# Block-diagonal product in a linear-attention kernel: 16 full matmuls replaced by four groups of 32x32 tile matmuls, woven into the last two q units

## Chip, cores and metric

One core of a Trainium2 chip. The metric is device microseconds of one execution of the whole program; 1 us of this program is 0.06%.

Three kinds of number appear. *Time* is a run's measured time. *Span* is that of the profiled run. *Stretch* is the distance between two instructions inside one trace. Several executions of one kernel differ by up to 1.5 us in time. A stretch repeats within about 0.03 us. Where less than 1.5 us is argued, the stretch is what counts. A *bubble* is time in which TensorE waits, and a *pack* is a group of 16 small matmuls that work side by side.

## The reference, cut to what matters

Two kinds of block alternate, attention (A) and a gated product (B), twice each. Only A is touched.

```python
def _A_ref(x, wqkv, wo):              # B, S, D = 1, 2048, 1024; H = 32 heads of Dh = 32
    qkv = ...                         # x @ wqkv, split by head
    pq, pk = phi(q), phi(k)
    kv = einsum("bhsd,bhse->bhde", pk, v)      # one 32x32 matrix per head
    num = einsum("bhqd,bhde->bhqe", pq, kv)
    den = ...
    return (num / den as B, S, D) @ wo
```

The kernel does not form `num`. It folds each head's 32x32 `kv` into that head's 32 rows of `wo`, giving M (1024x1024), and multiplies the normalised q by M. M is the product of a block-diagonal matrix with `wo`. Below, a q unit computes q for one tile of 128 rows, and an output unit multiplies one tile of the normalised q by M. TensorE writes to PSUM, which other engines must empty; a bank is a [128, 512] fp32 piece of it.

## The kernel before

`both` issues two matmuls, one for each half (512 columns) of a 1024-column output.

```python
def both(ps, lhsT, rhs, start, stop):
    for n in range(2):
        nc.tensor.matmul(out=ps[:, n, :], lhsT=lhsT, rhs=rhs[:, n * NB:(n + 1) * NB], start=start, stop=stop)

def g_unit(m):                     # G = xn^T phi(k), one block of 128 rows
    def run():
        ps = mm_tile()             # [128, 2, 512] fp32 in PSUM, two banks; three such buffers
        for t in range(NT):
            both(ps, XN[:, t, m * P:(m + 1) * P], PK[:, t, :], t == 0, t == NT - 1)
        nc.scalar.copy(out=Gs[m % 2], in_=flat(ps))
    return run

def kv_unit(m):                    # accumulates over m the diagonal 128x128 blocks: four heads each
    def run():
        ...                        # acc[0]: [P, KD, P] fp32
        for c in range(KD):
            nc.tensor.matmul(out=acc[0][:, c, :], lhsT=wkv[:, m, c * P:(c + 1) * P],
                             rhs=Gs[m % 2][:, c * P:(c + 1) * P], ...)
        if m == KD - 1:            # a mask of four 32x32 blocks of ones keeps the heads apart
            for h in range(2):
                nc.vector.tensor_tensor(out=KVb[:, 4 * h:4 * h + 4, :], in0=acc[0][:, 4 * h:4 * h + 4, :],
                                        in1=mask[:].unsqueeze(1).to_broadcast([P, 4, P]), op=ALU.mult)
    return run

def q_with_m(t, later):            # the last q unit, one pair of M matmuls per contraction step
    ...
    for c in range(KD):
        ...
        both(pm, KVb[:, c, :], wo[c], True, True)
        (nc.scalar.copy if c % 2 else nc.vector.tensor_copy)(out=M[:, c, :], in_=flat(pm))   # shortened
        step(c)                    # two matmuls of this q unit
    ...

# ... order of units at the end of a layer; d(t) is the division of tile t, VectorE work
do(... + [q[4]] + d(12) + [g[7], kv[6], q[5], kv[7], q[6]])
q_with_m(15, later)
...
do([out_unit(0)] + d(13) + [out_unit(1), out_unit(2)] + d(14) + [out_unit(3), out_unit(4)] + d(15))
```

## Time and profile before

| | before |
|---|---|
| time, median of 3 | 1630.27 us (1630.06 to 1630.41) |
| span of the profiled run | 1627.6 us |
| PE busy | 1622.9 us |
| 16 full matmuls (128x512) | 3.45 us, so 216 ns of TensorE each |
| stretch from the first kv 6 matmul to the first output unit | 14.70 us in both layers |

The page of the kernel before gives the busy time of each engine (in us, with its share of the span and the number of instructions), and further down the shares of the chain of work that ended last:

```profile
PE 1622.9 (100%) x7649; PEld 741.2 (46%) x7649; DVE 609.3 (37%) x889; ACT 289.3 (18%) x387; POOL 55.2 (3%) x141
...
PE 99%; DMA 0%; DVE 0%; issue 0%; SPq 0%
```

TensorE (PE) is busy throughout, and the chain is PE for 99%. The three waits of PE in the view of waits (what waited, for whom: us in total, times, longest) sum to 1.8 us:

```profile
PE ps L172 <- DVE xT L167: 1.2, 1, 1.2
PE ps L202 <- DVE xT L375: 0.3, 1, 0.3
PE pt L372 <- DVE R L359: 0.3, 1, 0.3
```

All are in the first 8 us. So only what TensorE gains or loses counts, and VectorE, 37% busy, matters only where TensorE must wait for it.

The next lines are the timeline of before at the end of the first attention layer. Columns: start in us, length in us, engine, line, operation, output <- inputs, shapes, count, and in brackets the idle time before and who ended it. DVE is VectorE, ACT is ScalarE.

```profile
165.75 0.61 PE L303 MATMUL kv<-GL,W 128*128 128x128 bf16 x8
...
166.00 1.01 ACT L293 CAST GL<-ps 128x1024 bf16<-128x1024 f32 x1 [5.02 <-PE ps L202]
...
166.19 3.62 PE L202 MATMUL ps<-W,xT 128*128 128x512 bf16 x16
...
167.67 1.23 DVE L284 TENSOR_TENSOR PQ<-PQ,den 128x1024 bf16<-128x1024 bf16 x1
...
169.65 0.61 PE L303 MATMUL kv<-GL,W 128*128 128x128 bf16 x8
170.09 3.62 PE L202 MATMUL ps<-W,xT 128*128 128x512 bf16 x16
...
170.29 1.29 DVE L308 TENSOR_TENSOR KVb<-kv,mask 128x512 bf16<-128x512 f32 x2 [1.40 <-PE kv L303]
...
173.54 0.59 PE L202 MATMUL pm<-W,KVb 128*128 128x512 bf16 x2
...
180.02 0.59 PE L202 MATMUL ps<-W,xT 128*128 128x512 bf16 x2
...
180.45 11.82 PE L202 MATMUL ps<-R,xT 128*128 128x512 bf16 x54
```

A shown length is not a slot. Each matmul is shown 379 ns long, but the 16 that begin at 166.19 are followed by the next unit at 169.65, so each holds TensorE for 216 ns. From 173.54 to 180.45 there are 32 matmuls in 6.91 us: dense, no bubble. Half of them make M. The fourth row is the last step of tile 12's division on VectorE, which ends at 168.90.

### The profile page before, as it was taken

To read this page: it belongs to the slowest core of one execution; us is meant where nothing else is said; L and a number is where in the kernel's file an instruction comes from. 1 tells how busy PE (TensorE), PEld (TensorE's weight loads), DVE (VectorE), ACT (ScalarE), POOL (GpSimd) and SP (SyncE) were. 2 spreads that over 40 slices of the span, in tenths; PEclk is the share of its full clock that TensorE was granted. 3 is DMA by queue.
4 is the path that set the end of the run, shared out by engine and by line. 5 is a ranking of instruction groups with operands and counts; after the bars stand their busy time and mean duration, and the time that the engine had idled before them with its cause. 6 is when DMAs were issued, how large, how long until landed. Compare 5 with 4: busy or idle time off the path is not lost.

```text
span 1627.6 us, 17734 instructions
## 1 busy us (share of the span) xinstructions
PE 1622.9 (100%) x7649; PEld 741.2 (46%) x7649; DVE 609.3 (37%) x889; ACT 289.3 (18%) x387; POOL 55.2 (3%) x141
## 2 busy tenths in 40 slices
PE   9999999999999999999999999999999999999999
PEld 4444444444444444444444444444444444444444
DVE  6889853212311321243245798432123113211111
ACT  5533201101110110011045222011011101101110
POOL 2100000000000000010000000000000000000000
PEclk9999999999999999999999999999999999999999
DMA  7324856511550452142420248565236406511400
GB/s 238 54 72 104 233 162 172 165 52 52 163 173 1 137 161 91 52 154 65 93 52 1 78 104 233 156 174 161 69 92 175 136 20 172 165 65 65 155 0 27
DMA packets 235742, 182.82 MB, mean 112 GB/s; under 512 B 101264, under 2 KB 216464, under 8 KB 235664
## 3 DMA queue, kind: packets, MB, share of 16 engines
q1 hardware_dynamic: 235664, 181.69, 39.0%
q8 instruction: 60, 0.98, 0.3%
q14 instruction: 18, 0.15, 0.0%
HBM read 153.09 MB, written 4.19 MB: 97 GB/s over the span
## 4 chain that ended last, share of the span: by engine, by line
PE 99%; DMA 0%; DVE 0%; issue 0%; SPq 0%
PE ps L202 50%; PE ps L489 48%; PE ps L516 1%; PE kv L303 0%; PE pm L202 0%; DMA X<-in_A_x_dram 0%; PE pt L372 0%; DVE xT L375 0%; DVE st L181 0%; DVE R L359 0%; SPq L107 0%; DVE X L497 0%; DVE mv L183 0%
## 5 line engine op out<-in xcount | busy, mean ns | idle before, releaser
L489 PE MATMUL ps<-xT,R 128*128 128x512 bf16 x2432 | 528.5, 379 | 0.0
L489 PEld LDWEIGHTS <-R 128*128 128x128 bf16 x2432 | 238.0, 98 | 286.9
L493 DVE TENSOR_TENSOR R<-gs,ps 128x512 bf16<-128x512 f32 x224 | 154.0, 687 | 533.4 <-ACT gs L492 533.4
L202 PEld LDWEIGHTS <-R 128*128 128x128 bf16 x2248 | 219.8, 98 | 264.3
L492 ACT COPY gs<-ps 128x512 f32<-128x512 f32 x224 | 131.3, 586 | 1039.2 <-PE ps L489 1039.2
L489 PE MATMUL ps<-xT,W 128*128 128x512 bf16 x1152 | 251.6, 379 | 0.0
L202 PEld LDWEIGHTS <-xT 128*128 128x128 bf16 x1536 | 149.6, 98 | 178.3 <-DVE xT L375 0.7
L202 PE MATMUL ps<-W,xT 128*128 128x512 bf16 x1024 | 225.9, 379 | 0.3 <-DVE xT L375 0.3
L489 PEld LDWEIGHTS <-W 128*128 128x128 bf16 x1152 | 112.7, 98 | 135.9
L202 PE MATMUL ps<-W,R 128*128 128x512 bf16 x744 | 170.7, 379 | 0.0
L497 DVE TENSOR_TENSOR X<-X,ps 128x1024 bf16<-128x1024 bf16 (+3 forms) x34 | 39.4, 1159 | 335.7 <-PE ps L202 326.0
L202 PE MATMUL ps<-R,R 128*128 128x512 bf16 x512 | 112.8, 379 | 0.0
L202 PE MATMUL ps<-PQ,R 128*128 128x512 bf16 x496 | 112.1, 379 | 0.0
L202 PE MATMUL ps<-R,xT 128*128 128x512 bf16 x512 | 110.8, 379 | 0.0
L207 ACT ACTIVATE e<-ps 128x1024 bf16<-128x1024 f32 x56 | 57.4, 1024 | 145.4 <-PE ps L202 145.4
L181 DVE BATCH_NORM_STATS2 st<-X 128x6 f32<-128x512 bf16 x128 | 82.0, 682 | 2.1 <-DMA X<-in_A_x_dram 1.9
L185 POOL TENSOR_SCALAR ve<-mv 128x1 f32<-128x1 f32 x64 | 16.7, 260 | 1332.3 <-DVE mv L183 1332.3
L202 PE MATMUL ps<-xT,R 128*128 128x512 bf16 x248 | 58.6, 379 | 0.0
L202 PE MATMUL ps<-GL,R 128*128 128x512 bf16 x248 | 58.6, 379 | 0.0
L343 DVE TENSOR_TENSOR X<-X,ps 128x1024 bf16<-128x1024 bf16 x32 | 38.8, 1213 | 28.0 <-PE ps L202 28.0
L192 DVE TENSOR_SCALAR R<-X,mv,rstd 128x1024 bf16<-128x1024 bf16 x64 | 33.9, 542 | 24.0 <-POOL rstd L187 24.0
L211 DVE TENSOR_SCALAR e<-e 128x1024 bf16<-128x1024 bf16 x64 | 27.0, 422 | 39.0 <-ACT e L207 39.0
(64 smaller groups left out, 459.9 us busy)
## 6 DMA issues: line engine op xcount, KB each, us to landing
R<-in_B_w_gate_dram SPq DMA_DIRECT2D x38, 1024.0 KB, 5.5
R<-in_B_w_up_dram SPq DMA_DIRECT2D x38, 1024.0 KB, 7.5
W<-in_B_w_gate_dram SPq DMA_DIRECT2D x18, 1024.0 KB, 5.4
W<-in_B_w_up_dram SPq DMA_DIRECT2D x18, 1024.0 KB, 7.3
W<-in_A_wqkv_dram SPq DMA_DIRECT2D x10, 1024.0 KB, 6.3
W<-in_B_w_down_dram SPq DMA_DIRECT2D x6, 1024.0 KB, 11.3
PQ<-in_B_w_down_dram SPq DMA_DIRECT2D x4, 1024.0 KB, 8.1
X<-in_A_x_dram SPq DMA_DIRECT2D x15, 256.0 KB, 5.4
```

Of the source, the lines that this page charges most:

```text
L181: nc.vector.bn_stats(out=st[:, c, :], in_=X[:, t, c * NB:(c + 1) * NB])
L185: nc.gpsimd.tensor_scalar(out=ve[:], in0=mv[:, 1:2], scalar1=1e-5, scalar2=None, op0=ALU.add)
L192: nc.vector.tensor_scalar(out=dst, in0=X[:, t, :], scalar1=mv[:, 0:1], scalar2=rstd[:], op0=ALU.subtract, op1=ALU.mult)
L202: nc.tensor.matmul(out=ps[:, n, :], lhsT=lhsT, rhs=rhs[:, n * NB:(n + 1) * NB], start=start, stop=stop)
L207: nc.scalar.activation(out=e[:], in_=flat(ps), func=ACT.Exp, **sc)
L211: nc.vector.tensor_scalar(out=e[:], in0=e[:], scalar1=1.0, scalar2=EPS, op0=ALU.min, op1=ALU.add)
L343: nc.vector.tensor_tensor(out=X[:, t, :], in0=X[:, t, :], in1=flat(ps), op=ALU.add)
L489: nc.tensor.matmul(out=ps[:, n, :], lhsT=w[:, k, j * P:(j + 1) * P], rhs=xT[g % 2][:, k, :], start=(k == 0), stop=(k == KD - 1))
L492: nc.scalar.copy(out=gs[:], in_=ps[:, 0, :])
L493: nc.vector.tensor_tensor(out=hT[:, f, :], in0=gs[:], in1=ps[:, 1, :], op=ALU.mult)
L497: nc.vector.tensor_tensor(out=X[:, t, a:b], in0=X[:, t, a:b], in1=ps, op=ALU.add)
L516: nc.tensor.matmul(out=ps[:, 0, 0:b - a], lhsT=hT[:, f, tl * P:(tl + 1) * P], rhs=wd[f][:, a:b], start=(f == 0), stop=(f == KF - 1))
```

## The change

The intent: `KVb` is three quarters zeros, and a full 128x128 matmul multiplies them. The array can be addressed as 16 independent tiles of 32x32 (the Trainium skill, "TensorEngine Tiling (Array Packing)", Tiling Modes), so one group of 16 small matmuls does the useful work of four full ones. To use all 16 tiles, `wo` is loaded with another row order and `KVb` is packed without zeros, by 16 small copies across partitions instead of two masked evictions. M is made in four quarters, between halves of the last two q units, so that each quarter's PSUM banks can be emptied before the next needs them. kv 7 moves ahead of q 13, to give the copies time, and the g units run one column half after the other so that the last G can be copied in halves.

```diff
-    KVb = const.tile([P, KD, P], BF16, tag="KVb", name="KVb")
+    KVb = const.tile([P, 2, 4, DH], BF16, tag="KVb", name="KVb")
...
-    wo_v = A_wo.rearrange("(k p) n -> p k n", p=P)
+    wo_v = A_wo.rearrange("(s r j e) n -> s r e j n", s=2, r=4, j=4)
... (output weights loaded in 8 DMAs of 32 partitions; mask removed)
         def g_unit(m):
             def run():
-                ps = mm_tile()
-                for t in range(NT):
-                    both(ps, XN[:, t, m * P:(m + 1) * P], PK[:, t, :], t == 0, t == NT - 1)
-                nc.scalar.copy(out=Gs[m % 2], in_=flat(ps))
+                for n in range(2):
+                    if n == 0 or m == KD - 1:
+                        ps = mm_tile()
+                    for t in range(NT):
+                        nc.tensor.matmul(out=ps[:, n, :], lhsT=XN[:, t, m * P:(m + 1) * P],
+                                         rhs=PK[:, t, n * NB:(n + 1) * NB], start=(t == 0), stop=(t == NT - 1))
+                    if m == KD - 1:
+                        nc.scalar.copy(out=Gs[m % 2][:, n * NB:(n + 1) * NB], in_=ps[:, n, :])
+                if m < KD - 1:
+                    nc.scalar.copy(out=Gs[m % 2], in_=flat(ps))
...                                      (kv_unit, at m == KD - 1; acc is now two tiles of one bank each)
-                        nc.vector.tensor_tensor(... mask ...)
+                    for r in range(4):
+                        copy = nc.scalar.copy if r // 2 else nc.vector.tensor_copy
+                        for j in range(4):
+                            copy(out=KVb[DH * r:DH * r + DH, :, j, :],
+                                 in_=acc[r // 2][DH * j:DH * j + DH, :, r % 2, DH * j:DH * j + DH])
...
-        def q_with_m(t, later):
-            ...
+        def last_q_with_m(later):
+            qs = [mm_tile(), mm_tile()]
+            wide = mm_tile()
+            bank = [psum.tile([P, NB], F32, tag=f"kv{i}", bufs=1, name="pm") for i in range(2)]
...                                      (steps(i, a, b): contraction steps a to b of q unit 14 + i)
+            def quarter(h, n, two):
+                for j in range(4):
+                    for r in range(4):
+                        o = bank[r][DH * j:DH * j + DH, :] if r < 2 else two[DH * j:DH * j + DH, r - 2, :]
+                        nc.tensor.matmul(out=o, lhsT=KVb[DH * r:DH * r + DH, h, j, :],
+                                         rhs=wo[h][DH * r:DH * r + DH, j, n * NB:(n + 1) * NB],
+                                         start=True, stop=True, tile_position=(DH * r, DH * j))
...                                      (quarter returns take, which copies banks to M)
+            take = quarter(0, 0, qs[1])
+            take(dve, 0)
+            take(dve, 1)
+            take(act, 2)
+            steps(0, 0, 4)
+            take = quarter(0, 1, wide)
...                                      (the same for quarters 3 and 4, then steps(1, 4, 8))
-        do(... + d(12) + [g[7], kv[6], q[5], kv[7], q[6]])
-        q_with_m(15, later)
+        do(... + d(12) + [g[7], kv[6], kv[7], q[5]])
+        last_q_with_m(later)
```

More of the change, by code (lines that the diff above doesn't have):

```diff
@@ L83 @@
     wq = rows(W2[:], D)
-    wo = [W3[:, c * D:(c + 1) * D] for c in range(4)] + [PQ[1][:, c * D:(c + 1) * D] for c in range(4)]
+    wo = [rows(W3[:], D), rows(PQ[1][:], D)]
     pq = [PQ[0][:, i * D:(i + 1) * D] for i in range(4)] + [PQ[1][:, i * D:(i + 1) * D] for i in range(4)]
@@ L123, in load_o @@
     def load_o(h):
-        load(rows((W3 if h == 0 else PQ[1])[:], D), wo_v[:, 4 * h:4 * h + 4, :])
+        for r in range(4):
+            load(wo[h][DH * r:DH * r + DH, :, :], wo_v[h, r])
     def load_gu(i):
@@ L153 @@
     nc.gpsimd.memset(ones[:], 1.0)
-    mask = const.tile([P, P], F32, tag="mask", name="mask")
-    nc.gpsimd.memset(mask[:], 0.0)
-    for b in range(P // DH):
-        nc.gpsimd.memset(mask[DH * b:DH * b + DH, DH * b:DH * b + DH], 1.0)
     warm = const.tile([P, 1], F32, tag="warm", name="warm")
@@ L300, in run @@
                 if m == 0:
-                    acc[:] = [psum.tile([P, KD, P], F32, tag="kv", bufs=1, name="kv")]
+                    acc[:] = [psum.tile([P, 2, 2, P], F32, tag=f"kv{i}", bufs=1, name="kv") for i in range(2)]
                 for c in range(KD):
-                    nc.tensor.matmul(out=acc[0][:, c, :], lhsT=wkv[:, m, c * P:(c + 1) * P],
+                    h, r = c // 4, c % 4
+                    nc.tensor.matmul(out=acc[r // 2][:, h, r % 2, :], lhsT=wkv[:, m, c * P:(c + 1) * P],
@@ L304, in run @@
                                      rhs=Gs[m % 2][:, c * P:(c + 1) * P],
-                                     start=(m == 0 and c % 4 == 0), stop=(m == KD - 1), skip_group_check=True)
+                                     start=(m == 0 and c in (0, 2)), stop=(m == KD - 1), skip_group_check=True)
                 if m == KD - 1:
-                    for h in range(2):
-                        nc.vector.tensor_tensor(out=KVb[:, 4 * h:4 * h + 4, :], in0=acc[0][:, 4 * h:4 * h + 4, :],
-                                                in1=mask[:].unsqueeze(1).to_broadcast([P, 4, P]), op=ALU.mult)
@@ L310, in kv_unit @@
-            return run
-        def q_with_m(t, later):
-            pss = [psum.tile([P, 2, NB], F32, tag="kv", bufs=1, name="pm"), mm_tile()]
-            ps = mm_tile()
-            pss.append(mm_tile())
-            tl = t % TPG
-            def step(c):
-                both(ps, xT[t // TPG][:, c, tl * P:(tl + 1) * P], wq[:, c, :], c == 0, c == KD - 1)
-            for c in range(KD):
-                if c == 2:
-                    step(c)
-                pm = pss[(0, 1, 0, 2, 1, 0, 2, 0)[c]]
-                both(pm, KVb[:, c, :], wo[c], True, True)
-                if c % 2:
-                    nc.scalar.copy(out=M[:, c, :], in_=flat(pm))
-                else:
-                    nc.vector.tensor_copy(out=M[:, c, :], in_=flat(pm))
-                if c != 2:
-                    step(c)
-                if c in (2, 4):
-                    later.pop(0)()
-            phi(ps, q_slot(t), scale_of(t))
+                    for r in range(4):
[3 more added lines that the diff above has]
+                                 in_=acc[r // 2][DH * j:DH * j + DH, :, r % 2, DH * j:DH * j + DH])
@@ new lines, in kv_unit, with steps, take @@
+            return run
+        def last_q_with_m(later):
+            qs = [mm_tile(), mm_tile()]
+            wide = mm_tile()
+            bank = [psum.tile([P, NB], F32, tag=f"kv{i}", bufs=1, name="pm") for i in range(2)]
+            def steps(i, a, b):
+                t = 14 + i
+                tl = t % TPG
+                for c in range(a, b):
+                    both(qs[i], xT[t // TPG][:, c, tl * P:(tl + 1) * P], wq[:, c, :], c == 0, c == KD - 1)
+            def quarter(h, n, two):
+                for j in range(4):
+                    for r in range(4):
+                        o = bank[r][DH * j:DH * j + DH, :] if r < 2 else two[DH * j:DH * j + DH, r - 2, :]
+                        nc.tensor.matmul(out=o, lhsT=KVb[DH * r:DH * r + DH, h, j, :],
+                                         rhs=wo[h][DH * r:DH * r + DH, j, n * NB:(n + 1) * NB],
+                                         start=True, stop=True, tile_position=(DH * r, DH * j))
+                def take(copy, r):
+                    cols = slice(n * NB, (n + 1) * NB)
+                    if r < 2:
+                        copy(out=M[:, 4 * h + r, cols], in_=bank[r][:])
+                    else:
+                        copy(out=M[:, 4 * h + 2:4 * h + 4, cols], in_=two[:])
+                return take
+            dve, act = nc.vector.tensor_copy, nc.scalar.copy
+            take = quarter(0, 0, qs[1])
[4 more added lines that the diff above has]
+            take = quarter(0, 1, wide)
+            take(dve, 0)
+            take(dve, 1)
+            take(act, 2)
+            steps(0, 4, 8)
+            take = quarter(1, 0, wide)
+            take(act, 0)
+            take(act, 1)
+            take(dve, 2)
+            phi(qs[0], q_slot(14), scale_of(14), later)
+            steps(1, 0, 4)
+            take = quarter(1, 1, wide)
+            take(dve, 0)
+            take(dve, 1)
+            take(dve, 2)
+            do(later)
+            steps(1, 4, 8)
+            phi(qs[1], q_slot(15), scale_of(15))
@@ L367, in turn_pe @@
                         continue
-                    tag, bufs = ("mm", 3) if h else ("kv", 1)
+                    tag, bufs = ("mm", 3) if h else ("kv0", 1)
                     pt = psum.tile([P, KD, P], BF16, tag=tag, bufs=bufs, name="pt")
@@ L450, in layer_A @@
         later = []
-        q[5], q[6] = q_unit(13, later), q_unit(14, later)
+        q[5] = q_unit(13, later)
         do([g[0], g[1], z_sum, kv[0]] + d(0) + [g[2], kv[1]] + d(1, 2) + [g[3], kv[2]] + d(3) + [q[0]] + d(4))
@@ L455, in layer_A @@
         load_o(1)
-        do(d(8) + [q[2], g[6], kv[5]] + d(9, 10) + [q[3]] + d(11) + [q[4]] + d(12) + [g[7], kv[6], q[5], kv[7], q[6]])
-        q_with_m(15, later)
+        do(d(8) + [q[2], g[6], kv[5]] + d(9, 10) + [q[3]] + d(11) + [q[4]] + d(12) + [g[7], kv[6], kv[7], q[5]])
+        last_q_with_m(later)
         load_gu(0)
```

## The prediction

> **What bounds the kernel now.** TensorE. The page gives PE 1622.9 of 1627.6 us busy; the chain of waits that ended last is 99% PE; PE's own waits sum to 1.8 us, all in the first 8 us. The chain lists 16 full matmuls (128x512) in 3.45 us: 216 ns each (the 379 ns shown overlap the next). So only PE time counts.
>
> **Removed.** Per attention layer (two of them) 16 full matmuls KVb x wo, 16 x 216 ns = 3.45 us. The timeline of before holds 32 matmuls in 6.91 us there (173.54 to 180.45 us), dense, so all of it is critical: 6.9 us in all. The masked evictions go too, off the path.
>
> **Added on PE.** Per layer four groups of 16 matmuls on 32x32 tiles, 512 columns each. The Trainium skill, "TensorE: Matmul & The Clock Gate", Part 3, gives the span of a pack as one matmul's duration plus about 4 ns per further tile; with the trace's 379 ns that is an estimate of 440 ns. "TensorEngine Tiling (Array Packing)", Key Properties, says changing the tiling mode drains TensorE; no trace shows one yet. I estimate the drain ahead of a group at 379-216 = 163 ns (the one behind it is in the 440). With 0.1 to 0.2 us for uncovered weight loads (98 ns each in the trace) a group costs about 0.75 us against the 0.86 us of the four matmuls it replaces: 0.45 us per layer. If weight-load/matmul pairs issue no faster than the 55 ns of the 128-column kv matmuls, a group costs 1.4 us, and the layer loses 2 us.
>
> **Moved.**
> 1. The last kv unit follows kv 6 at once. Its second half needs ScalarE's copy of the last half of G, which starts 0.25 us after the g unit and takes 0.59 us; 12 kv matmuls (0.66 us) cover it. Bubble 0.2 us per layer.
> 2. KVb comes from 16 small copies, half on VectorE, 0.15 to 0.2 us each. VectorE is behind there: tile 12's division ends 3.15 us after kv 6 starts, so the copies end at +4.4 to +4.8; q 13 ends near +4.5. Bubble 0 to 0.3 us before the first quarter.
> 3. Quarters are 8 full matmuls (1.73 us) apart; bank evictions (VectorE 0.65 us each, two in a row; ScalarE 1.0 us) end 0.3 us before the next quarter: no bubble.
> 4. g units run column half 0 first: PK of tile 15 is needed 3.24 us after the first g unit starts, and is ready 3.1 us after it. At most 0.1 us.
> 5. The output-weight load becomes 8 early DMAs: nothing.
>
> **Sum.** Per layer -3.45 + 4 x 0.75 + 0.2 + 0.1 = -0.15 us, twice: -0.3 us. I shade to -1 us, as the group may be shorter: **1629.3 us**, range 1626.3 to 1632.5. Faster by over 2%: 1%; within 2%: 98%; slower: 1% (all 6.9 us is only 0.4%).
>
> **What would show it.** In the timeline after, from the slot end of the last full matmul before a group to the start of the first after it: 0.75 us right, 0.4 us no drain paid, 1.4 us issue-bound. PE waits before kv 7 (0.2 us) and the first quarter (0 to 0.3 us), none before quarters two to four. g units unchanged at 6.91 us.
>
> **What would make it wrong.** A group's cost: each 0.1 us moves the total 0.8 us. Slow weight loads in tiled mode.

## The result

| | before | changed |
|---|---|---|
| time, median of 6 | 1630.16 us (1629.41 to 1630.41) | 1627.42 us (1627.19 to 1627.98) |
| span of the profiled run | 1627.6 us | 1625.4 us |
| stretch, first kv 6 matmul to first output unit, layers 1 and 2 | 14.70, 14.70 us | 13.77, 13.77 us |

The ratio is 0.9984, 95% interval 0.9972 to 0.9997: the same within 2%, and a little faster. A ratio is the mean time of one kernel's fast runs over that of the other's of the same rounds, so not quite the ratio of the medians quoted here. In later rounds, on chip 7, the unedited change took 1627.63 us against 1629.73 us (ratio 0.9987, 0.9974 to 0.9999). The two stretches give 2 x 0.93 = 1.86 us of the 2.1 to 2.7 us of the medians. In the two profiled runs, whose spans differ by 2.2 us, the rest is 0.07 us ahead of the first stretch and 0.26 us from the last addition on VectorE to the end of the span, where the last store is (2.59 against 2.33 us); neither is touched by the change, and both are of the size by which runs of one kernel differ.

The page of the changed kernel, its busy times and its chain:

```profile
PE 1620.7 (100%) x7745; PEld 738.9 (45%) x7745; DVE 612.4 (38%) x909; ACT 290.8 (18%) x405; POOL 54.5 (3%) x136
...
PE 94%; DVE 5%; issue 0%; ACT 0%; DVEq 0%
```

PE has 96 matmuls more (2 layers x (64 small less 16 full)) and is busy 2.2 us less. And the chain now runs through VectorE for 5%: TensorE is no longer the only engine that matters. That share is not what is lost: the chain follows VectorE's queue back from two short waits, some 40 us in each layer. The waits of PE in the changed kernel say where they are. The middle row is new:

```profile
PE ps L169 <- DVE xT L164: 1.2, 1, 1.2
PE pm L336 <- DVE KVb L315: 0.6, 2, 0.3
PE ps L199 <- DVE xT L411: 0.3, 1, 0.3
```

The timeline of the changed kernel over the same work (PEld is the weight load):

```profile
165.68 1.22 PE L307 MATMUL kv<-GL,W 128*128 128x128 bf16 x16
...
165.88 0.58 ACT L294 CAST GL<-ps 128x512 bf16<-128x512 f32 x1 [2.81 <-PE ps L291]
...
166.74 3.62 PE L199 MATMUL ps<-W,xT 128*128 128x512 bf16 x16
166.94 1.70 ACT L315 CAST KVb<-kv 32x64 bf16<-32x64 f32 x8 [0.47 <-PE kv L307]
...
167.60 1.23 DVE L281 TENSOR_TENSOR PQ<-PQ,den 128x1024 bf16<-128x1024 bf16 x1
168.74 1.85 DVE L315 CAST KVb<-kv 32x64 bf16<-32x64 f32 x8
...
170.65 0.24 PEld L336 LDWEIGHTS <-KVb 32*32 32x32 bf16 x16 [0.79 <-DVE KVb L315]
170.65 0.47 PE L336 MATMUL pm<-W,KVb 32*32 32x512 bf16 x2 [0.29 <-DVE KVb L315]
...
171.12 1.90 PE L199 MATMUL ps<-W,xT 128*128 128x512 bf16 x8
...
172.95 0.14 PEld L336 LDWEIGHTS <-KVb 32*32 32x32 bf16 x16 [0.42 <-issue]
172.95 0.39 PE L336 MATMUL pm<-W,KVb 32*32 32x512 bf16 x2
...
173.00 0.39 PE L336 MATMUL ps<-W,KVb 32*32 32x512 bf16 x2
...
173.31 1.41 PEld L199 LDWEIGHTS <-xT 128*128 128x128 bf16 x8 [0.23 <-issue]
173.32 1.90 PE L199 MATMUL ps<-W,xT 128*128 128x512 bf16 x8
...
179.45 6.85 PE L199 MATMUL ps<-R,xT 128*128 128x512 bf16 x31
```

Three things are read here.

*What a group costs.* From 171.12 to 173.32 there are eight full matmuls (8 x 216 = 1.73 us) and one group, so the group costs 2.20 - 1.73 = 0.47 us, against 4 x 216 = 864 ns for the four matmuls that it replaces. Of this, 0.10 us lies between the end of the last full slot (171.12 + 1.73 = 172.85) and the first tile; the 16 tiles start within 0.05 us; and the next full matmul follows 0.37 us after the first tile. Note the weight loads: they start together with their matmul at both changes (172.95 and 173.31), while inside a dense run they start some 0.2 us ahead (173.33 against 173.54 in the kernel before).

*The wait of kv 7.* 16 kv matmuls of 55 ns would take 0.88 us, and q 13 follows 166.74 - 165.68 = 1.06 us after the first. So 0.18 us are lost to the copy of G's last half. The single records of the trace show where: the 12th and the 13th kv matmul start 222 ns apart, and the 13th is the first that reads that half. The view of waits does not list it, since a kv matmul's shown length of 219 ns fills the gap.

*The wait ahead of quarter 1.* q 13 begins at 166.74 and its slots end at 170.19. The next full matmul comes at 171.12, 0.93 us later; the group accounts for 0.47 and 0.46 us are lost. The bracket says for whom: VectorE's KVb copies, which could start only at 168.74, when the division of tile 12 was done, and end at 170.59. (The view has 0.3 us per wait, because it counts from the shown end of the last matmul and not from the end of its slot.)

The sum per layer: -3.45 + 4 x 0.47 + 0.18 + 0.46 = -0.93 us, as the stretch shows.

### The profile page after: what moved, and what is told of

It is laid out like the page before. It is cut to its first block, busy times and chain, and to the rows that moved or that the text cites. A ratio compares the mean times of both kernels' runs of the same rounds, so it can differ in the third digit from the quotient of the medians.

```text
span 1625.4 us, 17975 instructions
## 1 busy us (share of the span) xinstructions
PE 1620.7 (100%) x7745; PEld 738.9 (45%) x7745; DVE 612.4 (38%) x909; ACT 290.8 (18%) x405; POOL 54.5 (3%) x136
## 4 chain that ended last, share of the span: by engine, by line
PE 94%; DVE 5%; issue 0%; ACT 0%; DVEq 0%
PE ps L525 48%; PE ps L199 41%; PE ps L291 3%; DVE den L277 1%; DVE PQ L281 1%; DVE tmp L275 1%; PE ps L552 1%; DVE PQ L209 0%; DVE den L280 0%; PE ps L169 0%; DVE den L279 0%; DVE KVb L315 0%; PE pm L336 0%; DVE e L208 0%; PE kv L307 0%
```

## The experiments

Theory T, drawn up from the changed kernel's trace: the gain is the tile groups' TensorE time. A visit to the tiled mode costs a fixed toll of about 0.25 us (entering and leaving), plus the streaming of 512 columns however many tiles share it (0.22 us); and two bubbles give part of the gain back. Rivals: the 0.47 us are the issue of 16 load/matmul pairs at 29 ns each (R1); the gain comes from the new schedule and not from tiles (R2); the late first quarter is a property of the tiled mode, not of VectorE (R3); bubbles add up (R4).

| run | edit, against the changed kernel | stretch, layers 1 and 2 (us) | time, median (us) | before in the same rounds |
|---|---|---|---|---|
| after_again | none | 13.74, 13.74 | 1627.63 | 1629.73 |
| untiled | full matmuls in the new schedule | 14.87, 14.87 | 1630.18 | 1629.94 |
| split8 | each group in two visits | 15.44, 15.44 | 1631.18 | 1629.94 |
| repeat2 | each group twice in a row | 14.62, 14.60 | 1629.32 | 1629.78 |
| repeat4 | each group four times in a row | 19.73, 17.15 | 1638.25 | 1629.94 |
| div12_later | tile 12's division later | 13.30, 13.30 | 1626.80 | 1629.94 |
| kv7_gap_only | a q 13 step ahead of kv 7 | 13.74, 13.74 | 1627.67 | 1629.73 |
| g_undone | g units as before | 14.00, 14.00 | 1628.11 | 1629.73 |
| both_bubbles | div12_later and kv7_gap_only | 13.14, 13.14 | 1626.81 | 1629.73 |

All gave the right result.

### after_again: the yardstick

No edit.

> The changed kernel once more, unedited, as the yardstick on the chip of the next three: stretch from the first kv 6 matmul to the first output unit 13.77 us in both layers, time about 2.5 us below before.

Measured: stretch 13.74 us twice, 2.1 us below before. This is the yardstick for the stretches below.

### untiled: the schedule without the tiles

```diff
             def quarter(h, n, two):
-                for j in range(4):
-                    for r in range(4):
-                        ... 32x32 tile matmul ...
+                for r in range(4):
+                    o = bank[r][:] if r < 2 else two[:, r - 2, :]
+                    nc.tensor.matmul(out=o, lhsT=KVb[:, 4 * h + r, :],
+                                     rhs=wo[4 * h + r][:, n * NB:(n + 1) * NB], start=True, stop=True)
  (KVb, its mask and the output-weight load as in the kernel before)
```

> The new schedule (order of kv 7, half-wise g units, quarters, evictions by banks) with the old full matmuls: masked KVb, four 128x512 matmuls per quarter. Theory A (the gain is TensorE time of the tiles): the stretch from the first kv 6 matmul to the first output unit is 14.7 to 14.9 us (before 14.70, changed 13.77), the time 1630 to 1630.6 us. Rival (the new schedule gives the gain, tiles are worth little): near 13.8 us and 1627.4 us.

Measured: 14.87 us in both layers, 1630.18 us, ratio to before 1.0002 (0.9987 to 1.0017). R2 falls: the schedule alone is 0.17 us per layer slower than before, which is kv 7's bubble (167.14 - 166.09 - 0.88 = 0.17 us), since PE shows no wait ahead of the quarters here. The masked evictions end at 170.44, before q 13's last slot ends (167.14 + 3.45 = 170.59):

```profile
167.14 3.62 PE L202 MATMUL ps<-W,xT 128*128 128x512 bf16 x16
...
169.16 1.28 DVE L315 TENSOR_TENSOR KVb<-kv,mask 128x512 bf16<-128x512 f32 x2
...
170.60 0.59 PE L335 MATMUL pm<-W,KVb 128*128 128x512 bf16 x2
```

Those lines are of this kernel's timeline. The tiles thus bring 14.87 - 13.74 = 1.13 us per layer net: 4 x (0.864 - 0.47) = 1.58 us of TensorE, less the 0.46 us wait that the slower KVb copies bring, make 1.12 us.

### split8: two visits of eight tiles

```diff
-            def quarter(h, n, two):
+            def quarter(h, n, two, i, c):
                 for j in range(4):
+                    if j == 2:
+                        one(i, c, 0)      # one full matmul of the q unit, moved here
                     for r in range(4):
```

> Each group of 16 is cut into two of 8 with one full matmul of the q unit between them (moved there, not added). Theory A (fixed toll per visit to the tiled mode, streaming of 0.22 us however many tiles): each half costs 0.44 to 0.47 us, so the total rises by 3.4 to 3.8 us. Theory B (29 ns per pair): each half costs about 0.24 us and the total stays within 0.3 us.

Measured: 1631.18 us, 3.6 to 3.8 us above the changed kernel's 1627.6 and 1627.4 us (other rounds). The timeline of this kernel, first visit and second visit around the one full matmul:

```profile
173.95 0.39 PE L344 MATMUL pm<-W,KVb 32*32 32x512 bf16 x2
...
174.29 0.39 PE L329 MATMUL ps<-W,xT 128*128 128x512 bf16 x1
174.61 0.39 PE L344 MATMUL pm<-W,KVb 32*32 32x512 bf16 x2
...
174.96 1.68 PE L329 MATMUL ps<-W,xT 128*128 128x512 bf16 x7
```

From 174.29 to 174.96 there are one slot of 0.216 us and one visit of eight tiles, 0.45 us, hardly less than the 0.47 us of 16. R1 falls: half the instructions do not halve the visit. T holds.

### repeat2 and repeat4: the same group several times

```diff
-                for j in range(4):
+                for j in [j for _ in range(4) for j in range(4)]:      # repeat2: range(2)
```

> Each group of 16 tile matmuls is issued four times in a row (same result; 24 extra packs in all). In the changed kernel a group takes 0.47 us from the end of the last full matmul's slot to the first full one after it. Theory A (a fixed toll of about 0.26 us for entering and leaving the tiled mode, and 0.22 us of streaming per pack, as for one full matmul): groups of 1.1 to 1.2 us, the total up by 5.2 to 6 us. Theory B (the issue of 16 load/matmul pairs at 29 ns each sets the 0.47 us): groups of 1.9 us, the total up by 11 us.

> Each group of 16 tile matmuls is issued twice in a row (8 extra packs in all). In repeat4 an extra pack cost 0.23 us inside a group, yet the total rose by 10.8 us for 24 packs, with holes in TensorE that the profile puts down to issue (2.0 us in one place). Theory (the holes come when the short tiled instructions outrun the supply of instructions, and with half as many per group they do not): groups of 0.70 us, the total 1.9 us above the changed kernel, no hole. Rival (a tiled pack costs 0.45 us in the total wherever it stands): 3.6 us above.

repeat2 was made because repeat4 missed both theories. Its timeline:

```profile
173.10 0.39 PE L336 MATMUL pm<-W,KVb 32*32 32x512 bf16 x2
...
173.33 0.38 PE L336 MATMUL pm<-W,KVb 32*32 32x512 bf16 x2
...
173.68 1.90 PE L199 MATMUL ps<-W,xT 128*128 128x512 bf16 x8
...
176.10 1.90 PE L199 MATMUL ps<-W,xT 128*128 128x512 bf16 x8
```

The period from 173.68 to 176.10 is 2.42 us against 2.20: a second pack of 16 in the same visit costs 0.22 us, the slot of one full matmul. The stretch rises by 0.86 to 0.88 us for four extra packs, the total by 1.7 us (1629.32 against 1627.63, different rounds) for eight. So the toll of a visit is 0.47 - 0.22 = 0.25 us, of which 0.05 us is the staggered start of 16 tiles, and the rest is 0.10 us on each side.

repeat4 holds to theory A inside a group and not in total. Most of its periods are 2.90 us (0.233 us for each extra pack, so groups of 1.17 us), but the total is 10.6 us above after_again (1638.25 against 1627.63 us, different rounds), where 24 x 0.233 = 5.6 were due. That this is near theory B's 11 us is chance. The largest piece is a hole in its fourth group:

```profile
180.64 0.37 PE L336 MATMUL ps<-PQ,KVb 32*32 32x512 bf16 x1
182.98 0.37 PE L336 MATMUL ps<-PQ,KVb 32*32 32x512 bf16 x1 [1.97 <-issue]
...
183.53 2.56 PE L199 MATMUL ps<-W,xT 128*128 128x512 bf16 x7 [0.16 <-issue]
...
185.89 1.49 PE L199 MATMUL ps<-R,xT 128*128 128x512 bf16 x3
```

The trace accounts for the rest. The hole costs 2.3 us by its starts (182.98 - 180.64). A second one, in the third group of layer 2, costs 0.6 us (992.18 to 992.81). And behind the first hole the granted clock is 0.5 from 184.17 to 187.58 us: there eight matmuls start 427 ns apart in place of 216 and cost 1.7 us. (Four of them stand in the last rows: the seven matmuls from 183.53 take 2.36 us, where 7 x 0.216 = 1.51 would do.) Together with the 5.6 us these make 10.2 us, and the profiled spans differ by 10.3 us (1636.1 against 1625.8). No other run shows a lowered clock inside its work; why it fell here was not tested.

No engine and no DMA released the instruction at 182.98; the profile calls that issue. A shortage of instructions after long runs of short ones would look like this, and repeat2, with half as many, shows no such hole. The trace also keeps the packets of a DMA queue that it calls instruction: one of 16 KB begins at 180.4 us, just ahead of the hole, and one at 990.3 us, 1.9 us ahead of the second. But in repeat2 such packets fall among the groups too (174.1 and 985.8 us), and there is no hole. So the cause is argued, not shown. The changed kernel shows no such loss: from the first kv 6 matmul of layer 1 to that of layer 2 there are 807.69 us in it (973.37 - 165.68) and 808.63 us before (974.38 - 165.75), and the difference of 0.94 us is that of the stretch alone.

### div12_later: free VectorE

```diff
-        do(... + [q[4]] + d(12) + [g[7], kv[6], kv[7], q[5]])
+        do(... + [q[4]] + [g[7], kv[6], kv[7], q[5]])
...
-        do([out_unit(0)] + d(13) + [out_unit(1), out_unit(2)] + d(14) + [out_unit(3), out_unit(4)] + d(15))
+        do([out_unit(0)] + d(12) + [out_unit(1), out_unit(2)] + d(13) + [out_unit(3), out_unit(4)] + d(14) + [out_unit(5)] + d(15))
```

> The division of tile 12 moves from before the g 7 unit to behind the first output unit, so VectorE is free when kv 7 ends. Theory: the 0.46 us that the first quarter loses is VectorE's backlog holding the KVb copies; then the wait goes, the stretch from kv 6 to the first output unit is 13.3 us, the total 0.9 us lower. Rival: the first visit to the tiled mode after a while is slow by itself (its first weight loads take longer): the 0.46 us stays.

Measured: 13.30 us twice, 1626.80 us, ratio to before 0.9981 (0.9966 to 0.9996). In the timeline of this kernel VectorE now idles until kv 7 is done, and the first group follows q 13 at once:

```profile
167.24 3.62 PE L199 MATMUL ps<-W,xT 128*128 128x512 bf16 x16
167.33 1.86 DVE L315 CAST KVb<-kv 32x64 bf16<-32x64 f32 x8 [2.37 <-PE kv L307]
...
170.78 0.39 PE L336 MATMUL pm<-W,KVb 32*32 32x512 bf16 x2
```

q 13's slots end at 167.24 + 3.45 = 170.69, and the group begins 0.09 us later, like every other group. R3 falls: the 0.46 us was VectorE's backlog. The time was expected to be 0.9 us lower than the changed kernel's and is 0.6 to 0.8 us lower by medians of other rounds. The division costs nothing in its new place: from kv 6 of layer 1 to that of layer 2 there are 807.23 us, 0.46 us less than in the changed kernel, as much as the stretch lost.

### kv7_gap_only, g_undone and both_bubbles: do the bubbles add up?

```diff
 kv7_gap_only
-        [g[7], kv[6], kv[7], q[5]]
+        [g[7], kv[6], q_13(0, 1), kv[7], q_13(1, KD)]     # q unit 13 in two pieces
 g_undone
-                for n in range(2): ...                    # column halves, two copies at the last m
+                for t in range(NT):
+                    both(ps, XN[:, t, m * P:(m + 1) * P], PK[:, t, :], t == 0, t == NT - 1)
+                nc.scalar.copy(out=Gs[m % 2], in_=flat(ps))
 both_bubbles = div12_later + kv7_gap_only
```

> Only the q 13 step moves between kv 6 and kv 7; tile 12's division stays where the change had it. Theory (the two bubbles are not additive, because the first quarter waits for VectorE, whose time is set by the division and not by TensorE): kv 7 no longer waits, q 13 ends 0.18 us earlier, the first quarter starts no earlier, the wait ahead of it grows by 0.18 us: the stretch stays at 13.7 to 13.8 us. Rival (bubbles add): 13.6 us and 0.36 us less in all.

> The g units go back to both column halves per weight and one full-width copy on ScalarE; all else as changed. kv 7 must then wait for a 1.0 us copy that starts 0.2 us after the g unit ends, behind 0.44 us of kv 6: bubble about 0.8 us in place of 0.18. Theory with the overlap of bubbles: q 13 then ends 0.66 us later, 0.2 us past the end of the KVb copies, so the first quarter no longer waits and the stretch grows by only 0.2 us, to about 14.0 us (0.4 us in all). Rival (bubbles add): 14.4 us, 1.3 us in all.

> Two edits: tile 12's division moves behind the first output unit (as in div12_later), and one contraction step (two full matmuls) of q 13 moves between kv 6 and kv 7. Theory: both bubbles (0.46 us ahead of the first quarter, 0.18 us ahead of kv 7's second half) go, the stretch is 13.13 us, the time 1.3 us below the changed kernel, the fastest of all.

The first two tell R4 apart. In kv7_gap_only kv 7 no longer waits, and the stretch is 13.74 us, to the hundredth what after_again shows. In g_undone kv 7 waits for a full-width copy, and the stretch is only 0.26 us longer (14.00). One row of each timeline, the first quarter of kv7_gap_only and then kv 7 of g_undone:

```profile
170.99 0.47 PE L347 MATMUL pm<-W,KVb 32*32 32x512 bf16 x2 [0.43 <-DVE KVb L326]
```

```profile
167.70 0.61 PE L301 MATMUL kv<-GL,W 128*128 128x128 bf16 x8 [0.71 <-ACT GL L290]
```

In the first, PE's shown idle time ahead of the quarter grew from 0.27 us (after_again) to 0.43 us: what kv 7 saved was waited out again. In the second the wait of kv 7 is about 0.87 us by its starts (167.70 less 166.39, less 0.44 us for kv 6), 0.69 us more than in the change, yet only 0.26 us of it shows, because TensorE would have waited for VectorE anyway. R4 falls: while VectorE's division sets the time of the copies, kv 7's bubble lies in its shadow.

both_bubbles takes both away. The stretch is 13.14 us, 0.60 us per layer below the change. The time is 1626.81 us against 1627.63 us of after_again in the same rounds, and 1629.73 us before (ratio 0.9981, 0.9968 to 0.9993). It has the shortest stretch of all. Expected were 1.3 us less than the change; the stretches give 1.2 us and the medians 0.8 us. In time it is not told apart from div12_later (1626.80 us, other rounds): the 0.16 us per layer between the two are below what runs of one kernel differ by.

## Why the prediction was right, and which of its terms were off

1. *The bound.* Right: TensorE is the bound, at most 6.9 us were to be had, the time stays within 2%. 1627.42 us lies within 1626.3 to 1632.5, though 1.9 us below the point of 1629.3. The range also holds the time of the kernel before, so that the number lies in it says little; the stretches test the terms.
2. *The price of a group: mis-sized.* Put at 0.75 us (0.163 for a drain, 0.44 for the span of the pack, 0.1 to 0.2 for weight loads), measured 0.47: 0.10 us ahead of the first tile and 0.37 us from there to the next full matmul, with nothing more for loads. The failed step is "I estimate the drain ahead of a group at 379-216 = 163 ns (the one behind it is in the 440)". A matmul's shown length of 379 ns was taken for time that a mode change must wait out. Shown lengths of matmuls are modelled, and nothing waited for them here: the first tile starts 0.10 us after the last full slot, and the next full matmul 0.37 us after the first tile, before the tiles' own shown end of 0.39. The two tolls of 0.10 us are of the size of one weight load (98 ns), and the loads start with their matmul there instead of ahead of it. When TensorE comes from a wait, with nothing to drain, the group still takes 0.47 us from its first load at 170.65 to the next full matmul at 171.12. That suggests an uncovered weight load on each side, in place of a drain. No run separates the two, so this stays open. The toll itself is shown by split8 and repeat2.
3. *Issue-bound groups (1.4 us): did not come.* 16 tiles start within 0.05 us.
4. *kv 7's wait.* Predicted 0.2 us, measured 0.18 us. What the prediction missed is that it costs nothing as long as the next wait covers it (kv7_gap_only).
5. *The wait ahead of the first quarter: mis-sized.* Predicted 0 to 0.3 us, entered with 0.1; measured 0.46. The cause was named rightly (tile 12's division; div12_later shows it). The copies were put at 0.15 to 0.2 us each and took 1.85 / 8 = 0.23 us, so they ended 4.91 us after kv 6 started, not 4.4 to 4.8.
6. *No wait ahead of quarters 2 to 4; g units unchanged; DMAs free.* Right: the PE waits list only two waits for KVb, one per layer, and the periods of 2.20 us are the same for all the groups.
7. *The sum.* Per layer -0.15 us was predicted and -0.93 us came: groups -1.12, the first quarter's wait +0.36, kv 7 -0.02. The shading to -1 us in all went the right way for a reason that was only guessed.

## What to carry to other kernels

Read the price of a matmul, and of a mode change, from distances between starts; the shown length of a matmul is not time that anything waits for. A visit to the 32x32 tiled mode here costs about 0.25 us whatever it holds, and 0.22 us for each pack of 512 columns, so collect packs in one visit as far as there is PSUM to take them; two in a row went as reckoned (repeat2), four brought holes (repeat4). And a change that frees the busiest engine can make its suppliers critical: see which queue the new operands wait in, and move what stands ahead of them, before a second bubble in the same shadow is worth mending.

## What the Trainium skill lacked or had wrong

- "TensorEngine Tiling (Array Packing)", Key Properties, says that changing the tiling mode drains TensorE, without a price. Here entering and leaving cost 0.10 us each, less than the 163 ns by which a full matmul's shown length exceeds its slot.
- The same page gives up to 16x for 32x32 tiles as a theoretical maximum, and "TensorE: Matmul & The Clock Gate", Part 3, a measured 10.6x for 16 tiles. Neither page says what packing gains where four full matmuls on a block-diagonal operand do the same work, nor what the first pack of a visit costs beyond a further one: here the first took 0.47 us in place of 0.86 (1.8x), and a further one 0.22 us (4x).
- "TensorE: Matmul & The Clock Gate", Part 3, puts a pack's span at one matmul plus about 4 ns per further tile. The trace agrees (172.95 to 173.39 us, 0.44 us). What it lacks is that the span is not what a pack costs here: the next full matmul starts 0.37 us after the first tile.
- The same part says, under what overlaps and what doesn't, that a weight load overlaps matmuls in flight only when its row group differs; the part's own account of the mechanism also allows for a background weight buffer. Here full 128-row loads of 98 ns run under full matmuls throughout (slots of 216 ns, a load for each).
- No page gives a case in which runs of tiled matmuls leave holes in TensorE: with 64 load/matmul pairs in each of eight groups two holes came, of 2.3 and 0.6 us (repeat4; cause not settled), with 32 none (repeat2).
- No page weighs gathering a block-diagonal operand by small copies across partitions against masking it: 0.23 us each on VectorE and 0.21 us on ScalarE for 32x64 elements, so 16 on two engines (1.85 us) took longer than two masked evictions of 128x512 (1.29 us).
